# Attention beside a feed-forward block on one core: a list planner's prices for GpSimd, its rule for row slices and its rule string are changed

## The chip, the cores and the metric

The kernel runs on one core of one Trainium2 chip. The metric is the device time of one execution, in microseconds; the time of before is the median of three runs. The engines are called as the profile calls them: PE (TensorE) with its weight loads PEld, ACT (ScalarE), DVE (VectorE), POOL (GpSimd) and SP (SyncE, which here issues nearly all transfers).

## What is computed

`x` is 2048 tokens of 640 values. The output is the sum of `x`, a multi-query attention over the normalised `x` (32 heads of 20 values that share one key and one value projection) and a feed-forward block of width 1728 over the same normalised `x`.

```python
def _A_ref(x, wq, wk, wv, wo):
    q = (lambda x, *d: x.transpose(*d))((x @ wq).reshape(B, S, H, Dh), 0, 2, 1, 3)
    k = x @ wk
    v = x @ wv
    scores = jnp.einsum("bhqd,bkd->bhqk", q, k) * (Dh ** -0.5)
    p = _softmax(scores, axis=-1)
    o = jnp.einsum("bhqk,bkd->bhqd", p, v)
    return (lambda x, *d: x.transpose(*d))(o, 0, 2, 1, 3).reshape(B, S, H * Dh) @ wo
def _B_ref(x, w1, w2):
    h = jnp.einsum("bsd,df->bsf", x, w1)
    h = _silu(h)
    out = jnp.einsum("bsf,fd->bsd", h, w2)
    return out
...
xn = _layernorm(x, axis=-1)
return x + _A_ref(xn, A_wq, A_wk, A_wv, A_wo) + _B_ref(xn, B_w1, B_w2)
```

## The kernel before

**Tiles.** The queries are cut into 4 chunks of 512 tokens and the 32 heads into 8 groups of 4, which gives 32 groups of work; in each, 16 tiles of 128 keys meet 4 heads of 512 queries. A score tile (`s_mm`, L1045) is one matmul of 32 rows by 128 columns into one PSUM bank; four of them, one for each head, can run side by side in the four row slots of the array. The weighted sum over the keys (PV, `pv_mms`, L1165) is four matmuls of 128 rows by 32 columns side by side, into bank 7. Weights times activations (queries, hidden layer, output) are column cuts in the same manner (`col_mm`, L427): four matmuls for one set. A **row slice** (`row_mm`, L434) is another way to do a quarter of such a set: one matmul of 32 rows by 128 columns that goes into a row slot which a score set leaves empty; four slices replace one column set.

**Two ways to the exponential.** ACT takes two or three banks of scores at a time with its exponential (L1130). For some key tiles of a group, a "batch" (`claim`, L1255), DVE and POOL do it instead: DVE adds a bias and rounds the scores into the bits of a bf16 number (p1, L1326, once for each head), and two copies shifted by constants are made of the four heads' result at once, a first shift s1 and a second s2. The second is always POOL's (L1365), the first is POOL's if its backlog is under `pj`, and else DVE's (L1370). Three PV sets with three versions of the values sum the three copies. So a batch takes 4 heads' tiles from ACT and adds two PV sets.

**The rest.** After the last key tile of a group the sums in bank 7 are copied out (L1213), their last row is turned round by transfers and a reciprocal (L820), POOL multiplies (the normalise, L829), and transfers pack the result. The query projections, the hidden layer (a tanh on ACT, L749, and a product on DVE, L752) and the output blocks (L871, and y at L886 for the last chunk) are fitted in between. At the end stand the sum (L966), its reciprocal (L969), the spread (L984), the product (L993), the last part of the output projection (`fin_job`, `fin_b`) and its eviction (L934).

**What sets the order.** Nothing is ordered by hand. `build` runs a list planner on the host with a clock for each engine: `Sched.est` gives the earliest start of an operation from what it depends on, `Sched.way` the time from the end of one operation to the start of another on a second engine, `Sched.commit` advances the clocks and the transfers' queue. An operation has a price `occ` on its engine and a latency `lat`. `port` marks the POOL operations and DVE shifts that share a memory port: `est` lets neither start before the other's `port_free`. The order that comes out is written to the engines with semaphores; on the chip each engine then runs its own list strictly in order. `step_pe` ranks PE's candidates; `row_slice` offers a slice only where the rule `ru.rows` allows a cut to be opened. Every 10 us of planned time (`PIECE`) one letter of the string `PLAN` chooses a deviation from the settings in `BASE` (`RULES`). The planner runs before the launch; none of its time is in the metric.

The prices that matter here, in ns: `POOL_SHIFT` 1900 for a shift and the default latency 60; 1350 + 200 for the normalise; 240 from POOL to PE; 600 or so for a p1.

Of the kernel before, what the change touches and what calls it, by code (L numbers as in the profile page):

```python
# [12 lines left out]
ALU = mybir.AluOpType  # L13

P = 128
D = 640
# [5 lines left out]
NG = H // HG  # L22
# [24 lines left out]
HALF = 320  # L47

LAT = 70.0
WAY = {("act", "dve"): 145.0, ("dve", "pool"): 10.0, ("pool", "pe"): 240.0}  # L50
WAY_E = 130.0
WAY_U = -50.0
WAY_DMA = -130.0
WAITS = 0.0
BUSY = 0.5
STRETCH = 2400.0
# [12 lines left out]
NG1 = 3  # L69
PA = 0.3  # L70
LOOKP = 1.0
POOL_SHIFT = 1900.0
POOL_J = (2,)
SWITCH = 85.0
SPRIO = 0.5
# [5 lines left out]
MARGIN = 200.0  # L81
# [9 lines left out]
ACT_LN = (5, 7)  # L91
TRACT = (0, 1)

BASE = dict(hold2=0, bnd=4, pj=4000.0, rows=1, rowmin=3, lagmax=6, lagp=0, lagj=6, openlag=5, late=-0.02, lead=0.01, leadmax=0.02, need=460.0, hold=300.0, dwant=600.0, slack=550.0, dnow=400.0, hungry=0.0, patience=0.0, keep=460.0, open=2, zcap=9, stay=0.0, homes=1, want=1, claim=6)
RULES = dict(a={}, b=dict(keep=0.0), c=dict(lagp=3), d=dict(lagp=5), e=dict(lagp=0), f=dict(patience=200.0), g=dict(dwant=0.0),
             h=dict(zcap=4), i=dict(zcap=3), j=dict(homes=0), k=dict(leadmax=-1.0, lead=-1.0), l=dict(lead=0.08, leadmax=0.1),
             m=dict(need=560.0), n=dict(hold=0.0), o=dict(stay=460.0), p=dict(open=1), q=dict(slack=400.0), r=dict(hungry=1000.0), s=dict(claim=9), t=dict(open=3), u=dict(claim=4), v=dict(want=2), w=dict(slack=700.0), x=dict(hold2=4), y=dict(bnd=0), z=dict(pj=-1e9), A=dict(rows=0), B=dict(rows=2, rowmin=2), C=dict(pj=2000.0), D=dict(openlag=3), E=dict(pj=8000.0), F=dict(hold2=3))
PLAN = "aaatadFcxxttxFzxBrtrAzgngmztnFaqEAEDaAqzirfDaaytFxFxrapAtznvqvndtnao"


def rule(n):
# [98 lines left out]
class Sched:  # L200
# [30 lines left out]
    def way(self, h, op):  # L231
        if h.eng == op.eng:
            return 0.0
        if h.dma_sem is not None:
            return WAY_DMA
        if op.eng == "pe" and op.mode == "p":
            if h.eng == "act":
                return WAY_E
            if h.eng == "dve" and h.name.startswith("Ucopy"):
                return WAY_U  # L240
        return WAY.get((h.eng, op.eng), LAT)

# [27 lines left out]
    def commit(self, op, start):  # L270
        e = op.eng
        op.deps = self.hazards(op)
        if op.sync is not None:
            op.deps.add(op.sync)
        op.start = start
        if e == "pe":
            if op.mode != self.pe_mode:
                start += SWITCH + (30.0 if op.mode == "p" else 20.0 if op.mode == "f" else 0.0)
                self.pe_mode = op.mode
            s0 = self.joined(op)  # L280
            if s0 is not None:
                end = max(start + op.occ, self.pe_set[2])
                self.pe_set = (s0, self.pe_set[1] | op.slots, end)
                op.fin = start + op.occ + 170.0
                op.occ = end - self.t[e]
                self.t[e] = end
            else:
                op.fin = start + op.occ + 170.0
                self.t[e] = start + op.occ
                self.pe_set = (start, op.slots, start + op.occ) if op.slots else None  # L290
        elif e == "sp":
            self.t[e] = start + op.occ
            own = 3300.0 if op.name == "dma wv" else 800.0 if op.name.startswith("dma pk") else 2000.0 if op.name.startswith("dma la") else 0.0
            self.dma_free = max(self.dma_free, start + 1300.0) + (op.lat - 800.0 if op.name.startswith("dma pk") else op.lat)
            op.fin = self.dma_free + 700.0 + own
        else:
            op.fin = start + op.occ + op.lat
            self.t[e] = start + op.occ
            if op.port:
                self.port_free[e] = start + op.occ  # L300
        op.done = True
        for r in op.reads:
            r.r.append(op)
        for r in op.writes:
            r.w = op
            r.r = []
        self.order[e].append(op)
        if op.on_commit is not None:
            op.on_commit(op)


def build(nc, A_x, A_wq, A_wk, A_wv, A_wo, B_x, B_w1, B_w2, out, stack):
    S = A_x.shape[1]
    F = B_w1.shape[1]
# [41 lines left out]
    U_sb = sb([P, 2, QW], F32)  # L356
# [7 lines left out]
    Rrep = nblk[:, 0:QW]  # L364
# [55 lines left out]
    def pool(fn, occ, lat=60.0, **kw):  # L420
        return sc.add(Op("pool", fn, occ, lat, **kw))
# [40 lines left out]
    def load_x(n):  # L462
# [12 lines left out]
               prio=0.04)  # L475
# [322 lines left out]
    pack_op = {}  # L798
# [12 lines left out]
    def norm_job(g, uc):  # L811

        qc, gi = divmod(g, NG)
        us, par = g % 2, qc % 2
        u0 = U_sb[DH:DH + 1, us, :]
        pu = u0.ap[0][0]
        la = dma(f"la{us}", lambda e: e.dma_start(
            Lg[:, us, :], bass.AP(U_sb, u0.offset, [[pu * SLOT, HG], [HG * QW // P, SLOT], [1, HG * QW // P]])), 8192,
            pre=[uc], reads=[res("U", us)], writes=[res("Lg", us)], prio=0.5)
        rc = dve(lambda v: v.reciprocal(rLg[:, us, :], Lg[:, us, :]), 160, pre=[la], reads=[res("Lg", us)],  # L820
                 writes=[res("rLg", us)], prio=0.1, name="recip")
        lb = dma(f"lb{us}", lambda e: e.dma_start(
            bass.AP(nblk, Rrow.offset, [[4 * Rrow.ap[0][0], HG], [HG * QW // P, SLOT], [1, HG * QW // P]]), rLg[:, us, :]),
                 8192, pre=[rc] + spread_op.get(g - 1, []), reads=[res("rLg", us)], writes=[res("Rrow")], prio=0.5)
        lc = [dma(f"lc{us}", lambda e, h=h: e.dma_start(Rrep[h * SLOT:(h + 1) * SLOT, :],
                                                        bass.AP(nblk, Rrow[4 * h:4 * h + 1, :].offset, [[Rrow.ap[0][0], 1], [0, SLOT], [1, QW]])),
                  5 * SLOT * QW * 4, pre=[lb] + [un_op[k] for k in [g - 1] if k in un_op], reads=[res("Rrow")], writes=[res("Rrep", h)], prio=0.5) for h in range(HG)]
        spread_op[g] = lc
        nm = pool(lambda e: e.tensor_tensor(oU[:, us, :], U_sb[:, us, :], Rrep, ALU.mult), 1350.0 + MARGIN, pre=[uc] + lc + pack_op.get(divmod(g - 2, NG), []),  # L829
                  reads=[res("U", us)] + [res("Rrep", h) for h in range(HG)], writes=[res("oU", us)], prio=0.1)  # L830
        un_op[g] = nm
        nm.port = True
        nm.gate = calm(nm)
        packs = []
        for i in range(HG):
            row = (gi * HG + i) * DH
            lo = i * SLOT
            left = DH
            while left:
                c, r = divmod(row, P)  # L840
                n = min(left, P - r)
                o = dma(f"pk{us}", lambda e, c=c, r=r, n=n, lo=lo: e.dma_start(oT[r:r + n, par, c, :], oU[lo:lo + n, us, :]),
                        n * QW * 2 + 200000, pre=[nm] + ([kT_op[k] for k in range(KT)] + q_op[0] if qc == 1 else []), reads=[res("oU", us)], writes=[res("oT", par, gi, i, c)], prio=0.6)
                o.gate = lambda: oT_free(qc)
                packs.append(o)
                row, lo, left = row + n, lo + n, left - n
        pack_op[(qc, gi)] = packs
# [203 lines left out]
    def plan(n):  # L1051
# [17 lines left out]
        if w[2] is None or w[2][0] < need - ru.hold:  # L1069
# [3 lines left out]
    RUNLIST = {k: [tuple(range(a, a + (k - 1) * d + 1, d)) for d in range(1, STEPS + 1) for a in range(UB - (k - 1) * d)]  # L1073
               for k in (2, 3)}

    def left_over(banks, gone):

        return sum(all(b in banks and b not in gone for b in r) for r in RUNLIST[3])

    e_owner = [None] * NSLOT  # L1080
    e_next = [0]
# [255 lines left out]
    def dve_advance(job):  # L1337
# [14 lines left out]
        for j in range(1, NJ):  # L1352
# [10 lines left out]
            args = dict(pre=st["p1"] + ([idb] + [norm_op[n] for n in range(NT)] if old is None else [old] if isinstance(old, Op) else [old["pv"][j]]), reads=zr, writes=[r], name=f"s{j}")  # L1363
            if j in POOL_J or pool_load() < ru.pj:
                op = pool(lambda v, t=t, j=j, zin=zin: v.tensor_scalar(t.bitcast(I16), zin, float(SHIFT[j]), 1.0, ALU.add, ALU.mult),  # L1365
                          POOL_SHIFT, prio=0.3, **args)
                op.port = True
                op.gate = calm(op)
            else:
                op = dve(lambda v, t=t, j=j, zin=zin: v.tensor_scalar_add(t.bitcast(I16), zin, float(SHIFT[j])), t_dve(N, 4),  # L1370
                         prio=SPRIO - 0.01 * j, **args)
                op.port = True
                op.on_commit = shifts.append
# [354 lines left out]
    def dve_idle(t):  # L1728
# [3 lines left out]
                return False  # L1732
        return True

    def lag_now():
        pend = [n for n in e_users if exp_ops[n].done and any(o is None or not o.done for o in e_users[n])]
        return att["n"] - min(pend) if pend else 0

    def step_pe():
        t = sc.t["pe"]  # L1740
# [40 lines left out]
        if ru.stay and mode != "s" and not pro and t + 230.0 < act_until(att["n"]) - ru.stay:  # L1781
            order.remove("s")
            order.insert(len(order) - 1, "s")
        if not make_s_act() and all(not u for u in unclaimed):
            order = ["p", "pd", "d", "r", "m0", "m", "l", "s"]
        order += ["z", "x"]
        if ru.bnd and att["pgroup"] < NGR and pv_left[att["pgroup"]] <= ru.bnd and not pro:
# [268 lines left out]
```

## Time and profile before

| | before |
|---|---|
| median of 3 runs, us | 700.38 (699.88 to 700.77) |
| the profiled execution, us | 700.23 |
| its span, first to last instruction, us | 698.3 |
| granted TensorE clock | 1.00 throughout |
| read from HBM, written to HBM | 11.09 MB, 2.62 MB |

In the profile's groups a row holds the line, the engine, the operation, output and input with their shapes and the count; then the busy time in us and the mean ns of one; then the idle time just before the group's instructions, with what ended it. A stretch's row holds the busy us of PE, PEld, DVE, ACT and POOL, each with its count of instructions, then the clock, the transfers' share and GB/s. A row of the waits is "who waited <- for whom: us in total, times, longest". A timeline row is the start, the length from the first start to the last end, and what ran how often. An instruction's duration runs to the end of its last write, so on ACT, DVE and PE the next one may start before it ends.

### The profile page before, as it was taken

What the parts mean: (1) busy time and instruction counts of PE and PEld (TensorE: products, weight loads), DVE (VectorE), ACT (ScalarE), POOL (GpSimd) and SP (SyncE); (2) the same over time, 40 slices, a digit from 0 to 9 for tenths busy, and PEclk for the clock granted to TensorE, in tenths of its full rate; (3) what the DMA queues carried; (4) which work ended last, traced back from release to release, by engine and by line L of the source; (5) the groups of instructions that cost most, each with busy time, mean ns of one, the idle gap of its engine ahead of it and who ended that gap; (6) DMA issues with size and microseconds to landing.
All of it is one profiled execution on the core that took longest, in us unless ns stands there. A gap on an engine that the chain in (4) does not pass through costs nothing.

```text
span 698.3 us, 22678 instructions
## 1 busy us (share of the span) xinstructions
PE 683.0 (98%) x9927; PEld 228.4 (33%) x9927; DVE 572.4 (82%) x969; ACT 679.4 (97%) x735; POOL 584.4 (84%) x351
## 2 busy tenths in 40 slices
PE   8999999999999999999999999999999999999997
PEld 5422222222232433322223333322223233333344
DVE  7788788899898668988898888788899798778763
ACT  6899999999999999999999999999999999999994
POOL 6658999989985976989988679999888997999991
PEclk9999999999999999999999999999999999999999
DMA  7643220222211222231122221232222022232201
GB/s 219 186 163 41 19 21 22 31 28 28 22 14 18 38 39 33 35 65 18 23 22 29 29 29 24 30 74 30 28 19 22 9 31 32 32 67 22 23 7 40
DMA packets 34242, 28.99 MB, mean 42 GB/s; under 512 B 15486, under 2 KB 29662, under 8 KB 34142
## 3 DMA queue, kind: packets, MB, share of 16 engines
q1 hardware_dynamic: 33854, 27.20, 25.3%
q8 instruction: 78, 1.28, 0.8%
q10 hardware_dynamic: 288, 0.33, 0.1%
q14 instruction: 22, 0.18, 0.1%
HBM read 11.09 MB, written 2.62 MB: 20 GB/s over the span
## 4 chain that ended last, share of the span: by engine, by line
PE 43%; ACT 42%; POOL 7%; DVE 5%; DMA 2%; issue 1%; SPq 0%; DVEq 0%; POOLq 0%; ACTq 0%
ACT sbt L1130 40%; PE psall L1165 15%; PE psall L1045 14%; PE psall L427 12%; POOL sbt L1365 7%; DVE sbt L1326 2%; ACT sbt L749 2%; DVE sbt L1370 1%; DMA sbt<-in_A_x_dram 1%; DMA sbt<-sbt 1%; PE psall L601 1%; DVE sbt L934 0%; PE psall L966 0%; DVE sbt L1213 0%; PE psall L984 0%
## 5 line engine op out<-in xcount | busy, mean ns | idle before, releaser
L1130 ACT ACTIVATE sbt<-psall 128x1024 bf16<-128x1024 f32 (+1 forms) x663 | 657.6, 1215 | 3.0 <-PE psall L1045 2.3
L1365 POOL TENSOR_SCALAR sbt<-sbt 128x2048 int16<-128x2048 int16 x275 | 521.7, 1897 | 76.1 <-DVE sbt L1326 25.3
L1326 DVE TENSOR_SCALAR sbt<-psall 128x512 int16<-128x512 f32 x648 | 427.1, 684 | 90.5 <-PE psall L1045 74.5
L1045 PE MATMUL psall<-sbt 32*128 32x512 bf16 x2048 | 271.6, 385 | 4.5 <-ACT sbt L1130 1.3
L1165 PE MATMUL psall<-sbt 128*32 128x512 bf16 x3344 | 270.7, 385 | 4.0 <-POOL sbt L1365 1.5
L427 PE MATMUL psall<-sbt 128*32 128x320 bf16 (+3 forms) x3664 | 221.4, 331 | 0.3 <-DVE sbt L1326 0.2
L1045 PEld LDWEIGHTS psall<-sbt 32*128 32x128 bf16 x2048 | 72.0, 91 | 248.0 <-ACT sbt L1130 190.7
L1165 PEld LDWEIGHTS psall<-sbt 128*32 128x32 bf16 x3344 | 66.4, 94 | 120.7 <-issue 82.1
L427 PEld LDWEIGHTS psall<-sbt 128*32 128x32 bf16 (+1 forms) x3664 | 79.9, 95 | 76.3 <-issue 45.7
L434 PE MATMUL psall<-sbt 32*128 32x320 bf16 (+1 forms) x240 | 81.4, 339 | 0.4
L829 POOL TENSOR_TENSOR sbt<-sbt 128x512 bf16<-128x512 f32 x30 | 38.2, 1274 | 11.6 <-DVE sbt L1370 6.6
L1370 DVE TENSOR_SCALAR sbt<-sbt 128x2048 int16<-128x2048 int16 x49 | 43.1, 894 | 0.6 <-PE psall L1165 0.5
L752 DVE SCALAR_TENSOR_TENSOR sbt<-sbt,psall 128x512 bf16<-128x512 bf16 x52 | 35.5, 683 | 6.8 <-ACT sbt L749 5.7
L749 ACT ACTIVATE sbt<-psall 128x512 bf16<-128x512 f32 x52 | 39.4, 757 | 0.1
L434 PEld LDWEIGHTS psall<-sbt 32*128 32x128 bf16 x240 | 21.8, 91 | 2.9 <-PE psall L434 2.1
L1213 DVE COPY sbt<-psall 128x512 f32<-128x512 f32 x31 | 21.2, 682 | 0.5 <-PE psall L1165 0.3
L1638 PE MATMUL psall<-sbt 128*32 128x256 bf16 (+1 forms) x296 | 19.8, 365 | 1.2 <-DVE sbt L467 1.2
L672 DVE TENSOR_SCALAR sbt<-psall 128x512 bf16<-128x512 f32 x20 | 13.7, 683 | 1.1 <-PE psall L434 0.5
L871 DVE SCALAR_TENSOR_TENSOR sbt<-psall,sbt 128x320 bf16<-128x320 f32 x24 | 11.6, 481 | 0.6 <-PE psall L1045 0.6
L565 POOL TENSOR_SCALAR sbt<-sbt 128x640 bf16<-128x640 bf16 x12 | 10.4, 874 | 1.7 <-DVE sbt L557 1.4
L552 POOL TENSOR_TENSOR sbt<-sbt 128x2 f32<-128x2 f32 x8 | 5.5, 693 | 6.7 <-DVE sbt L550 6.7
L1638 PEld LDWEIGHTS psall<-sbt 128*32 128x32 bf16 x296 | 8.1, 110 | 6.8 <-issue 3.2
(63 smaller groups left out, 110.6 us busy)
## 6 DMA issues: line engine op xcount, KB each, us to landing
sbt<-sbt SPq DMA_DIRECT2D x120, 64.0 KB, 3.9
sbt<-in_A_x_dram SPq DMA_DIRECT2D x28, 160.0 KB, 3.9
sbt<-sbt SPq DMA_DIRECT2D x213, 20.0 KB
out_dram<-sbt SPq DMA_DIRECT2D x14, 160.0 KB, 3.0
sbt<-in_B_w_dram SPq DMA_DIRECT2D x1, 2160.0 KB, 11.7
sbt<-in_B_w_dram SPq DMA_DIRECT2D x1, 2080.0 KB, 8.3
sbt<-sbt SPq DMA_DIRECT2D x75, 8.0 KB
sbt<-in_A_wq_dram SPq DMA_DIRECT2D x1, 800.0 KB, 7.5
```

The costliest lines, as they stand in the source:

```text
L427: ins = pe.matmul(ps[j * SLOT:(j + 1) * SLOT, b * BANK + off:b * BANK + off + n], w[:, j * SLOT:(j + 1) * SLOT], x, start=start, stop=stop ...
L434: return pe.matmul(ps[0:w.shape[-1], b * BANK:b * BANK + n], w[k], x[k], start=start, stop=stop, tile_position=(r * SLOT, 0))
L749: t = Op("act", lambda a: a.activation(t_buf[0:rows, ts, :], bk(job.bank, 0, QW, rows=rows), AF.Tanh, scale=0.5), t_act(512), 215, pre=[jo ...
L752: u = Op("dve", lambda v: v.scalar_tensor_tensor(out=hT[par][0:rows, fk, :], in0=t_buf[0:rows, ts, :], scalar=1.0, in1=bk(job.bank, 0, QW, ...
L829: nm = pool(lambda e: e.tensor_tensor(oU[:, us, :], U_sb[:, us, :], Rrep, ALU.mult), 1350.0 + MARGIN, pre=[uc] + lc + pack_op.get(divmod(g ...
L1045: return pe.matmul(bk(b), kT_rep[i * SLOT:(i + 1) * SLOT, kt * P:(kt + 1) * P], qT[i * SLOT:(i + 1) * SLOT, g % NQ, :], start=True, stop=T ...
L1130: return a.activation(Ebuf[:, es * QW:es * QW + w], ps[:, buf[0] * BANK:buf[0] * BANK + w], AF.Exp, scale=ESCALE)
L1165: ins = pe.matmul(ps[i * SLOT:(i + 1) * SLOT, UB * BANK:UB * BANK + QW], lhsT, rhs, start=(first and k < HG), stop=(last and k >= len(lst) ...
L1326: p1 = Op("dve", lambda v: v.tensor_scalar(z16[:, i * QW:(i + 1) * QW], bk(job.bank), ZBIAS, 0.0, ALU.add, ALU.max), t_dve(QW) + 2.0, 140, ...
L1365: op = pool(lambda v, t=t, j=j, zin=zin: v.tensor_scalar(t.bitcast(I16), zin, float(SHIFT[j]), 1.0, ALU.add, ALU.mult), POOL_SHIFT, prio=0 ...
L1370: op = dve(lambda v, t=t, j=j, zin=zin: v.tensor_scalar_add(t.bitcast(I16), zin, float(SHIFT[j])), t_dve(N, 4), prio=SPRIO - 0.01 * j, **args)
L1638: ins = pe.matmul(ps[i * SLOT:(i + 1) * SLOT, UB * BANK:UB * BANK + n], zero_t[:, 0:SLOT], zero_t[:, 0:n], start=fresh, stop=fresh, tile_p ...
```

## The change

The planner's prices for POOL are replaced: a shift 1976 without latency in place of 1900 with 60, the normalise 1356 in place of 1550, 160 from POOL to a PV or column set (`WAY_S`) in place of 240 to any PE operation. The shared port counts as free 79 ns (`PORT_GAP`) before a POOL operation's slot ends, and a DVE operation that waited for the port is 53 ns (`PORT_HID`) cheaper. In `BASE`, `rows` goes from 1 to 0, so that slices are offered only in stretches whose letter is `B` (as before, two open cuts) or the new `G` (one), and `pj` goes from 4000 to 6000. `PLAN` is another string of 68 letters, with 8 `B` and 3 `G`. `left_over`, `lag_now` and one test in `step_pe` are written to run faster on the host.

```diff
-WAY = {("act", "dve"): 145.0, ("dve", "pool"): 10.0, ("pool", "pe"): 240.0}
+WAY = {("act", "dve"): 145.0, ("dve", "pool"): 10.0}
...
+WAY_S = 160.0
+PORT_GAP = 79.0
+PORT_HID = 53.0
...
-POOL_SHIFT = 1900.0
+POOL_SHIFT = 1976.0
...
-BASE = dict(hold2=0, bnd=4, pj=4000.0, rows=1, ...
+BASE = dict(hold2=0, bnd=4, pj=6000.0, rows=0, ...
...
-...  F=dict(hold2=3))
-PLAN = "aaatadFcxxttxFzxBrtrAzgngmztnFaqEAEDaAqzirfDaaytFxFxrapAtznvqvndtnao"
+...  F=dict(hold2=3), G=dict(rows=1))
+PLAN = "aaanGtxBBExhEhmxadrBBzraCBBEGqtrztfFzrqhwnpofocotyxddmGjvmpBaBitntqo"
...
         if op.eng == "pe" and op.mode == "p":
             if h.eng == "act":
                 return WAY_E
+            if h.eng == "pool":
+                return WAY_S
...
+            if op.port and e == "dve" and start > self.t[e] and start <= self.port_free["pool"] + 1.0:
+                op.occ -= PORT_HID
             op.fin = start + op.occ + op.lat
             self.t[e] = start + op.occ
             if op.port:
-                self.port_free[e] = start + op.occ
+                self.port_free[e] = start + op.occ - (PORT_GAP if e == "pool" else 0.0)
...
-        nm = pool(lambda e: e.tensor_tensor(oU[:, us, :], U_sb[:, us, :], Rrep, ALU.mult), 1350.0 + MARGIN, ...
+        nm = pool(lambda e: e.tensor_tensor(oU[:, us, :], U_sb[:, us, :], Rrep, ALU.mult), 1356.0, ...
...
-                          POOL_SHIFT, prio=0.3, **args)
+                          POOL_SHIFT, 0.0, prio=0.3, **args)
...
-        pend = [n for n in e_users if exp_ops[n].done and any(o is None or not o.done for o in e_users[n])]
-        return att["n"] - min(pend) if pend else 0
+        n, base = att["n"], lag_base[0]
+        while base < n and exp_ops[base].done and all(o is not None and o.done for o in e_users[base]):
+            base += 1
+        lag_base[0] = base
+        for k in range(base, n):
+            if exp_ops[k].done and any(o is None or not o.done for o in e_users[k]):
+                return n - k
+        return 0
```

What the two built programs hold, counted by instruction; every other instruction, each transfer among them, is there as often in both, and nearly all stand in another order from about the 40th microsecond on:

| instruction (line before) | before | after |
|---|---|---|
| ACT exponential of 2 banks, of 3 banks (L1130) | 589, 74 | 573, 82 |
| DVE p1 (L1326) | 648 | 656 |
| DVE first shifts (L1370) | 49 | 49 |
| POOL first shifts, second shifts (L1365) | 113, 162 | 115, 164 |
| PE row slices of 320 columns, of 512 (L434) | 136, 104 | 32, 28 |
| PE column matmuls of 320 columns, of 512 (L427) | 2184, 1372 | 2288, 1448 |
| PE matmuls of PV (L1165) | 3344 | 3360 |
| PE fillers of 256 columns, of 512 (L1638) | 156, 140 | 148, 116 |

More of the change, by code (lines that the diff above doesn't have):

```diff
@@ L92 @@
 TRACT = (0, 1)
-BASE = dict(hold2=0, bnd=4, pj=4000.0, rows=1, rowmin=3, lagmax=6, lagp=0, lagj=6, openlag=5, late=-0.02, lead=0.01, leadmax=0.02, need=460.0, hold=300.0, dwant=600.0, slack=550.0, dnow=400.0, hungry=0.0, patience=0.0, keep=460.0, open=2, zcap=9, stay=0.0, homes=1, want=1, claim=6)
+BASE = dict(hold2=0, bnd=4, pj=6000.0, rows=0, rowmin=3, lagmax=6, lagp=0, lagj=6, openlag=5, late=-0.02, lead=0.01, leadmax=0.02, need=460.0, hold=300.0, dwant=600.0, slack=550.0, dnow=400.0, hungry=0.0, patience=0.0, keep=460.0, open=2, zcap=9, stay=0.0, homes=1, want=1, claim=6)
 RULES = dict(a={}, b=dict(keep=0.0), c=dict(lagp=3), d=dict(lagp=5), e=dict(lagp=0), f=dict(patience=200.0), g=dict(dwant=0.0),
              h=dict(zcap=4), i=dict(zcap=3), j=dict(homes=0), k=dict(leadmax=-1.0, lead=-1.0), l=dict(lead=0.08, leadmax=0.1),
-             m=dict(need=560.0), n=dict(hold=0.0), o=dict(stay=460.0), p=dict(open=1), q=dict(slack=400.0), r=dict(hungry=1000.0), s=dict(claim=9), t=dict(open=3), u=dict(claim=4), v=dict(want=2), w=dict(slack=700.0), x=dict(hold2=4), y=dict(bnd=0), z=dict(pj=-1e9), A=dict(rows=0), B=dict(rows=2, rowmin=2), C=dict(pj=2000.0), D=dict(openlag=3), E=dict(pj=8000.0), F=dict(hold2=3))
-PLAN = "aaatadFcxxttxFzxBrtrAzgngmztnFaqEAEDaAqzirfDaaytFxFxrapAtznvqvndtnao"
+             m=dict(need=560.0), n=dict(hold=0.0), o=dict(stay=460.0), p=dict(open=1), q=dict(slack=400.0), r=dict(hungry=1000.0), s=dict(claim=9), t=dict(open=3), u=dict(claim=4), v=dict(want=2), w=dict(slack=700.0), x=dict(hold2=4), y=dict(bnd=0), z=dict(pj=-1e9), A=dict(rows=0), B=dict(rows=2, rowmin=2), C=dict(pj=2000.0), D=dict(openlag=3), E=dict(pj=8000.0), F=dict(hold2=3), G=dict(rows=1))
+PLAN = "aaanGtxBBExhEhmxadrBBzraCBBEGqtrztfFzrqhwnpofocotyxddmGjvmpBaBitntqo"
 def rule(n):
@@ L828, in norm_job @@
         spread_op[g] = lc
-        nm = pool(lambda e: e.tensor_tensor(oU[:, us, :], U_sb[:, us, :], Rrep, ALU.mult), 1350.0 + MARGIN, pre=[uc] + lc + pack_op.get(divmod(g - 2, NG), []),
+        nm = pool(lambda e: e.tensor_tensor(oU[:, us, :], U_sb[:, us, :], Rrep, ALU.mult), 1356.0, pre=[uc] + lc + pack_op.get(divmod(g - 2, NG), []),
                   reads=[res("U", us)] + [res("Rrep", h) for h in range(HG)], writes=[res("oU", us)], prio=0.1)
@@ L1074, in build @@
                for k in (2, 3)}
+    RUN3 = [frozenset(r) for r in RUNLIST[3]]
     def left_over(banks, gone):
-        return sum(all(b in banks and b not in gone for b in r) for r in RUNLIST[3])
+        left = set(banks).difference(gone)
+        return sum(r <= left for r in RUN3)
     e_owner = [None] * NSLOT
@@ L1733, in dve_idle @@
         return True
+    lag_base = [0]
     def lag_now():
-        pend = [n for n in e_users if exp_ops[n].done and any(o is None or not o.done for o in e_users[n])]
-        return att["n"] - min(pend) if pend else 0
+        n, base = att["n"], lag_base[0]
[6 more added lines that the diff above has]
+        return 0
     def step_pe():
@@ L1783, in step_pe @@
             order.insert(len(order) - 1, "s")
-        if not make_s_act() and all(not u for u in unclaimed):
+        if all(not u for u in unclaimed) and not make_s_act():
             order = ["p", "pd", "d", "r", "m0", "m", "l", "s"]
```

## Prediction

> **What bounds the kernel now.** I read the page's head first, then the groups of instructions by line with shapes apart, the busy time by stretches, the table of waits, and the timeline where a price was wanted.
>
> ```profile
> span 698.3 us, 22678 instructions
> PE 683.0 (98%) x9927; PEld 228.4 (33%) x9927; DVE 572.4 (82%) x969; ACT 679.4 (97%) x735; POOL 584.4 (84%) x351
> ...
> 400.00:500.00 100.00, 99.31 (x1478) 32.41 (x1478) 81.95 (x133) 100.00 (x108) 89.69 (x50) 1.00 0.27 37
> ...
> L1130 ACT ACTIVATE sbt<-psall 128x1024 bf16<-128x1024 f32 x589 | 571.8, 1170 | 1.9 <-PE psall L1045 1.2
> L1130 ACT ACTIVATE sbt<-psall 128x1536 bf16<-128x1536 f32 x74 | 113.8, 1578 | 1.2 <-PE psall L1045 1.1
> ...
> PEld psall L1045 <- ACT sbt L1130: 190.7, 501, 0.8
> PEld psall L1165 <- issue: 82.1, 364, 0.2
> ```
>
> Two engines look full. PE's 98% is spread over pipelined matmuls, so it doesn't say that PE is the limit. The waits decide: 501 times the weight load of a score set (L1045) stood until ACT's exponential (L1130) gave up PSUM banks, 190.7 us in all. Even a wait that nothing causes ("issue") lasts 82.1/364 = 0.226 us, the change of tile shape; without it about 190.7 - 501 x 0.226 = 77 us are left in which PE had nothing to do but wait for ACT. ACT, on the other hand, is busy in every us of the stretch from 400 to 500. ACT sets the pace from the first exponential to the last.
>
> But "busy" on ACT counts an instruction's latency too; the mean of 1170 ns is not the step from one to the next. That step comes from the timeline of ACT:
>
> ```profile
> 13.93 5.98 ACT sbt L1130 x5
> ...
> 86.86 3.07 ACT L1130 ACTIVATE sbt<-psall 128x1024 bf16<-128x1024 f32 x3
> 89.58 0.85 ACT L749 ACTIVATE sbt<-psall 128x512 bf16<-128x512 f32 x1
> 90.05 2.21 ACT L1130 ACTIVATE sbt<-psall 128x1024 bf16<-128x1024 f32 x2
> 91.86 0.89 ACT L749 ACTIVATE sbt<-psall 128x512 bf16<-128x512 f32 x1
> ...
> 680.26 8.35 ACT L1130 ACTIVATE sbt<-psall 128x1536 bf16<-128x1536 f32 x6
> ```
>
> A pair of banks takes (91.86 - 90.05)/2 = 0.905 us, a tanh (L749) 0.47. Three banks: (8.35 - 1.58)/5 = 1.354 from this row, 0.905 + (1.578 - 1.170) = 1.313 from the two means; I take 1.33. From the first exponential (13.93) to the end of the last (680.26 + 8.35 = 688.61) are 674.7 us. The steps add to 589 x 0.905 + 74 x 1.33 + 54 x 0.47 + about 2 for the three projections = 658.9. So ACT loses about 15.8 us to late score sets, a loss that the idle column (1.9 + 1.2) hardly shows. The span is: 13.9 before, 658.9 of steps, 15.8 of loss, 9.7 behind.
>
> **ACT's work (the two more batches).** By the built order ACT issues 573 pairs and 82 triples: -16 x 0.905 + 8 x 1.33 = **-3.8 us**, on the path. This is the surest term. Eight heads' tiles move to DVE and GpSimd (on GpSimd 162 to 164 second shifts and 113 to 115 first ones; DVE keeps 49 shifts), whose prices are:
>
> ```profile
> 133.00 15.73 POOL L1365 TENSOR_SCALAR sbt<-sbt 128x2048 int16<-128x2048 int16 x8
> 656.05 2.47 DVE L1326 TENSOR_SCALAR sbt<-psall 128x512 int16<-128x512 f32 x4
> L1365 POOL TENSOR_SCALAR sbt<-sbt 128x2048 int16<-128x2048 int16 x275 | 521.7, 1897 | 76.1 <-DVE sbt L1326 25.3 <-DVE sbt L1370 16.9 <-PE psall L1165 8.1
> L1370 DVE TENSOR_SCALAR sbt<-sbt x49: 673/820/2328, 54.9 to 661.4; 128x2048 int16<-128x2048 int16 x49
> ```
>
> GpSimd's step is (15.73 - 1.90)/7 = 1.976 us, so four more shifts are +7.9; DVE's is (2.47 - 0.68)/3 = 0.60, so eight more first passes are +4.8. Both lie beside ACT: GpSimd has 698 - 584 = 114 us idle, DVE 126. Were that cover gone, as in the stretch at 133 where GpSimd runs eight shifts without a gap, a late shift holds the PV matmul that wants it and with it all that is queued on PE.
>
> **PE (slices only by rule).** 180 row slices of 1 matmul go, 26 + 19 column cuts of 4 matmuls come.
>
> ```profile
> 661.21 0.39 PE L1045 MATMUL psall<-sbt 32*128 32x512 bf16 x3
> 661.22 0.30 PE L434 MATMUL psall<-sbt 32*128 32x320 bf16 x1
> 661.53 0.40 PE L1165 MATMUL psall<-sbt 128*32 128x512 bf16 x4
> ...
> 666.19 1.05 PE L1165 MATMUL psall<-sbt 128*32 128x512 bf16 x16
> 680.02 1.13 PE L427 MATMUL psall<-sbt 128*32 128x320 bf16 x28
> ```
>
> The slice starts 10 ns after the score set and is over before it: it costs PE nothing, and taking it away frees nothing. The cuts cost stream time: (1.05 - 0.40)/3 = 0.217 us for 4 matmuls of 512 columns, hence 0.137 for 320. So 26 x 0.137 + 19 x 0.217 = +7.7; 16 more PV matmuls +0.9; 8 fewer fillers of 256 and 24 of 512 columns -1.5; 654 contiguous stretches of score work become 649, each some 0.44 (0.32 to the next kind, as 661.21 to 661.53, and 0.12 back), -2.2. Net +4.9 us for PE, which lies under the 77 us of waiting for ACT on the average; without that cover it would be all on the path.
>
> **The tail.** The built order puts the last y blocks behind the last exponentials, so more of the final projection (L427) is left behind the last spread (L984): 124 matmuls for 72.
>
> ```profile
> 690.97 1.05 PE L984 MATMUL psall<-sbt 128*32 128x128 f32 x32
> 691.84 2.77 PE L427 MATMUL psall<-sbt 128*32 128x512 bf16 x72
> 692.59 3.08 DVE L934 SCALAR_TENSOR_TENSOR sbt<-psall,sbt 128x512 bf16<-128x512 f32 x5
> ```
>
> At 0.217 us for 4 x 512 columns the 124 stream 4.6 us (9 sets each of 512, 384 and 256, 4 of 128), the 72 stream 2.5. PE ends at 691.84 + 2.77 = 694.6 and the last eviction starts at 692.59 + 4 x 0.6 = 695.0; 2.1 later on PE makes that 696.7: **+1.7**. Bounds 0 (if those matmuls fill waits for L969 and L993) and +2.1.
>
> **The loss of 15.8 us.** The new numbers (1.976 for the shift, the port free 79 ns before its slot ends, 1.356 for the normalise, 160 ns to PE) stand close to the rows: 1.976, 1.976 - 1.897 = 0.079. The old 1.900 was short by 76 ns a shift, and the trace has what follows:
>
> ```profile
> PEld psall L1165 <- POOL sbt L1365: 12.5, 37, 0.8
> PE psall L1165 <- POOL sbt L1365: 1.5, 5, 0.4
> 658.12 0.10 PEld L1165 LDWEIGHTS psall<-sbt 128*32 128x32 bf16 x4 [0.62 <-POOL sbt L1365]
> ```
>
> Of 14.0 us in 42 waits, 42 x 0.226 are the change of shape; 4.5 us are GpSimd being late, the most that better numbers can give back there. The other bound is +7.7: every new column cut in a place where PE has no lead. Counted in the two built orders with the prices above, score sets whose stretch of PE work outlasts the exponential it lies under are 199 before and 184 after, so I stay near the first bound: **-2**. The planner's quicker counting of lag and runs changes nothing that runs; transfers are as many as before. The first 40 us are ordered as before but for a few PE rows.
>
> Sum: -3.8 + 1.7 - 2 = -4.1 us on 700.23 us of the profiled execution (span 698.3 and 1.9 around it), 0.15 under the median of the runs shown, 700.38. Forecast **696.3 us**, -0.6%.
>
> **Rules of the Trainium skill.** The L1370 row has shifts on DVE from 673 to 2328 ns for one shape, and a run that began beside a GpSimd shift shows why: DVE stands until it ends. The Trainium skill (SBUF — State Buffer, Who interferes with whom) says that whichever of the two issues first holds the shared ports for its whole instruction and the other fully blocks, so issue order decides, not a constant in the planner. The trace agrees in the 2328 ns. By that rule alone the 53 ns that the new planner takes off such a wait would be worth nothing, and the collision rival below takes the place of my -2.
>
> PE's row of 98% would, taken at its word, put the +4.9 us on the path. The Trainium skill (Perfetto Trace Analysis, Identifying the Most-Contended Engine) says that matmul busy time is no good measure for TensorE, and to use the load of weights' share; that is 33% here. By the row (PE the limit, ACT's saving worth nothing) the sum would be 4.9 + 1.7 = +6.6, by the rule -4.1.
>
> **Rivals.**
> - *The stalls go.* All 4.5 us of GpSimd's lateness vanish from ACT's loss: -3.8 + 1.7 - 4.5 = -6.6, 693.8 us. For it: the 76 ns. Against: PE waits for ACT at 501 of some 650 sets, so most lateness on PE is taken up there.
> - *No gain left.* The plan is new in nearly all of its 68 stretches, and the loss grows by about 2 elsewhere: -3.8 + 1.7 + 2 = -0.1, 700.3 us. The change then doesn't do what it says.
> - *Column cuts on the path (slower).* A slice went under a score set for nothing; as a column cut it stands between two score sets. If two thirds of 7.7 fall where PE has no lead, -3.8 + 1.7 + 5.1 = +3.0, 703.4 us. It decides from 2.1/7.7 = 27% on. For it: 0.905 us for a pair leaves only 0.905 - 0.44 = 0.46 for two PV sets or three cuts. Against: the 77 us.
> - *Collisions (slower).* A DVE shift that meets a GpSimd shift head-on costs 2.33 - 0.67 = 1.66 us, less one exponential of lead (0.9) is 0.75 on ACT. Ten more of these in the new order: -3.8 + 1.7 + 7.5 = +5.4, 705.8. DVE issues 49 shifts as before, which speaks against it.
>
> **Chances.** Forecast 0.48, the stalls go 0.12, no gain left 0.15, column cuts 0.18, collisions 0.07. Less than 0.2% (1.4 us) can't be told from no change by these measurements. So faster 0.60, same 0.15, slower 0.25. The forecast's own range is 693.5 (loss -4.5, tail +1.6) to 699 (loss +0.5, tail +2.1). The whole range goes from 691, where some lateness of DVE goes too, to 703.5, which takes in the column cuts and leaves out the collisions.
>
> **What would show it.** ACT with 573 + 82 exponentials and steps of 0.905 and 1.33 between them; about 669 us from the first exponential to the end of the last where it had 674.7; the last exponential's end to the end of the span 11.4 where it had 9.7; fewer than 42 waits of L1165's counterpart for GpSimd. I am wrong if the sum of ACT's steps falls by 3.8 and the stretch doesn't: then the loss has grown, and the waits in front of the score sets name the engine; or if the tail grows by more than 2.1.

## The result and the profile after

The changed kernel takes 693.92 us in the median (four runs, 693.9 to 694.29) where the kernel before took 700.18 beside it: ratio 0.9911, 95% interval 0.9894 to 0.9928, or 6.3 us less. 696.3 was forecast, within a range of 691.0 to 703.5; the time lies closest to the rival in which GpSimd's lateness goes (693.8).

The page of the changed kernel, its head and the groups that answer to those of before (L1140 is L1130 of before, L1375 is L1365):

```profile
span 692.1 us, 22655 instructions
...
PE 680.5 (98%) x9908; PEld 229.7 (33%) x9911; DVE 572.0 (83%) x977; ACT 673.5 (97%) x727; POOL 593.0 (86%) x355
...
L1375 POOL TENSOR_SCALAR sbt<-sbt 128x2048 int16<-128x2048 int16 x279 | 530.5, 1901 | 62.7 <-DVE sbt L1380 12.7
```

The row of DVE's own shifts alone (count, then the least, median and longest duration in ns; L1370 of before had 673/820/2328):

```profile
L1380 DVE TENSOR_SCALAR sbt<-sbt x49: 630/697/2065, 64.3 to 654.1; 128x2048 int16<-128x2048 int16 x49
```

The groups by line with shapes apart, then the table of waits:

```profile
L1140 ACT ACTIVATE sbt<-psall 128x1024 bf16<-128x1024 f32 x573 | 555.0, 1172 | 0.3
...
L1140 ACT ACTIVATE sbt<-psall 128x1536 bf16<-128x1536 f32 x82 | 124.6, 1555 | 1.9 <-PE psall L1052 1.7
```

```profile
PEld psall L1052 <- ACT sbt L1140: 194.9, 503, 0.8
...
PEld psall L1175 <- POOL sbt L1375: 9.5, 35, 0.6
```

ACT still sets the pace: 503 score sets waited for it, as before 501. PV waits for GpSimd 35 times and 9.5 us where it was 42 times and 14.0; beyond 0.226 us for each change of shape that is 1.6 us, down from 4.5. GpSimd does four more shifts and idles 62.7 us before them where it idled 76.1. The median of DVE's own shifts fell from 820 to 697 ns: 17 of the 49 took over 0.8 us where 26 did, so fewer of them stood long behind a GpSimd shift.

Next come rows from ACT's timeline at both ends of the exponentials, then the chip's end from the timeline of all engines:

```profile
12.84 2.37 ACT L1140 ACTIVATE sbt<-psall 128x1536 bf16<-128x1536 f32 x2
...
676.59 4.31 ACT L1140 ACTIVATE sbt<-psall 128x1536 bf16<-128x1536 f32 x3
```

```profile
683.97 4.82 PE L434 MATMUL psall<-sbt 128*32 128x384 bf16 x124
685.23 1.36 DVE L941 SCALAR_TENSOR_TENSOR sbt<-psall,sbt 128x512 bf16<-128x512 f32 x2 [0.59 <-PE psall L434]
687.20 0.69 DVE L941 SCALAR_TENSOR_TENSOR sbt<-psall,sbt 128x512 bf16<-128x512 f32 x1 [0.60 <-PE psall L434]
688.19 1.34 DVE L941 SCALAR_TENSOR_TENSOR sbt<-psall,sbt 128x512 bf16<-128x512 f32 x2 [0.30 <-PE psall L434]
```

The exponentials end at 676.59 + 4.31 = 680.90, which leaves 11.2 us of tail where 9.7 were. The 124 matmuls take 4.82 us behind the spread (2.77 for 72 before), and DVE now waits for PE three times among the five evictions (0.59, 0.60 and 0.30 us), where it ran five without a gap.

The span can be cut as the prediction cut it: the start of the first exponential; ACT's steps (0.905 for a pair, 1.33 for a triple, 0.47 for a tanh, 2 for the projections); what the stretch from the first to the end of the last exponential holds beyond them, the loss; the tail, from there to the end of the span. All kernels of this study side by side, in us (the steps of the two kernels with act16 are those of before less 3.8; each ratio is to runs of before made beside that kernel). The intervals reach 0.0009 to 0.0017 to either side, 0.6 to 1.2 us, so a smaller difference between two rows is not shown by the times alone.

| kernel | median, or ratio to before [95%] | span | first | steps | loss | tail | PV's waits for GpSimd's shifts (PEld) |
|---|---|---|---|---|---|---|---|
| before | 700.18 | 698.3 | 13.9 | 658.9 | 15.8 | 9.7 | 12.5 in 37 |
| after | 0.9911 [0.9894, 0.9928] | 692.1 | 12.8 | 655.0 | 13.1 | 11.2 | 9.5 in 35 |
| b_shift490 | 0.9968 [0.9956, 0.9979] | 695.7 | 13.0 | 658.9 | 14.0 | 9.7 | 3.9 in 17 |
| a_shift490 | 0.9911 [0.9896, 0.9926] | 691.8 | 13.0 | 655.0 | 12.6 | 11.2 | 3.6 in 16 |
| b_shift256 | 0.9970 [0.9958, 0.9982] | 695.6 | 12.9 | 658.9 | 14.1 | 9.7 | 2.5 in 11 |
| a_shift256 | 0.9906 [0.9892, 0.9921] | 691.8 | 13.3 | 655.0 | 12.3 | 11.2 | 5.0 in 22 |
| b_slice64 | 0.9999 [0.9990, 1.0009] | 698.1 | 13.1 | 658.9 | 16.3 | 9.8 | |
| a_tail | 0.9903 [0.9888, 0.9918] | 691.4 | 13.1 | 655.0 | 12.9 | 10.4 | |
| a_cols | 0.9892 [0.9877, 0.9907] | 690.4 | 12.9 | 655.0 | 11.5 | 11.1 | |
| b_cols | 0.9981 [0.9972, 0.9991] | 696.5 | 12.8 | 658.9 | 15.1 | 9.7 | |
| b_act16 | 0.9989 [0.9980, 0.9999] | 697.3 | 13.1 | 655.1 | 19.3 | 9.7 | 15.5 in 41 |
| b_act16_shift490 | 0.9924 [0.9907, 0.9941] | 693.7 | 13.1 | 655.1 | 15.8 | 9.7 | 4.3 in 18 |
| p_newprices | 1.0058 [1.0042, 1.0074] | 702.2 | 13.0 | 662.3 | 15.7 | 11.2 | 7.5 in 29 |
| p_oldprices | 1.0203 [1.0186, 1.0220] | 712.6 | 12.8 | 664.0 | 26.2 | 9.6 | 22.0 in 59 |

From before to after the span falls by 6.2: first -1.1, steps -3.9, loss -2.7, tail +1.5. The first term isn't the plan's: in the profile of before ACT stood 1.00 us for a transfer of x ahead of its first statistics, in no other. The run b_slice64, as long as before, began at 13.1 and lost 16.3, so about half of that 1.1 only moves into the loss.

### The profile page after: what moved, and what is told of

Read it like the earlier page. It is cut to its first block, busy times and chain, and to the rows that moved or that the text cites. A ratio compares the mean times of both kernels' runs of the same rounds, so it can differ in the third digit from the quotient of the medians.

```text
span 692.1 us, 22655 instructions
## 1 busy us (share of the span) xinstructions
PE 680.5 (98%) x9908; PEld 229.7 (33%) x9911; DVE 572.0 (83%) x977; ACT 673.5 (97%) x727; POOL 593.0 (86%) x355
## 4 chain that ended last, share of the span: by engine, by line
ACT 57%; PE 35%; DVE 5%; POOL 3%; issue 1%; DMA 0%
ACT sbt L1140 53%; PE psall L434 11%; PE psall L1175 11%; PE psall L1052 11%; ACT sbt L756 3%; POOL sbt L1375 2%; DVE sbt L1336 1%; DVE sbt L552 1%; DVE sbt L550 1%; DVE sbt L594 1%; POOL sbt L836 0%; DMA sbt<-in_A_x_dram 0%; PE psall L608 0%; PE psall L973 0%; DVE sbt L679 0%
## 5 line engine op out<-in xcount | busy, mean ns | idle before, releaser
L1140 ACT ACTIVATE sbt<-psall 128x1024 bf16<-128x1024 f32 (+1 forms) x655 | 652.5, 1220 | 2.2 <-PE psall L1052 1.7
L1375 POOL TENSOR_SCALAR sbt<-sbt 128x2048 int16<-128x2048 int16 x279 | 530.5, 1901 | 62.7 <-DVE sbt L1380 12.7
L1052 PE MATMUL psall<-sbt 32*128 32x512 bf16 x2048 | 265.9, 384 | 3.7 <-ACT sbt L1140 1.8
L1175 PE MATMUL psall<-sbt 128*32 128x512 bf16 x3360 | 267.7, 384 | 1.2 <-DVE sbt L1223 0.4
L434 PE MATMUL psall<-sbt 128*32 128x320 bf16 (+2 forms) x3844 | 226.6, 331 | 0.7 <-ACT sbt L1140 0.5
L1052 PEld LDWEIGHTS psall<-sbt 32*128 32x128 bf16 x2048 | 70.0, 91 | 248.8 <-ACT sbt L1140 194.9
L434 PEld LDWEIGHTS psall<-sbt 128*32 128x32 bf16 x3844 | 83.9, 95 | 77.7 <-issue 46.9
L1175 PEld LDWEIGHTS psall<-sbt 128*32 128x32 bf16 x3360 | 66.0, 94 | 115.1 <-issue 82.4
L1380 DVE TENSOR_SCALAR sbt<-sbt 128x2048 int16<-128x2048 int16 x49 | 39.8, 827 | 0.2
L441 PE MATMUL psall<-sbt 32*128 32x320 bf16 (+1 forms) x60 | 20.5, 342 | 0.1
L893 DVE SCALAR_TENSOR_TENSOR sbt<-psall,sbt 128x320 f32<-128x320 f32 x8 | 3.9, 485 | 9.8 <-PE psall L434 9.7
L572 POOL TENSOR_SCALAR sbt<-sbt 128x640 bf16<-128x640 bf16 x12 | 10.4, 878 | 1.5 <-DVE sbt L564 1.2
L1648 PEld LDWEIGHTS psall<-sbt 128*32 128x32 bf16 x264 | 7.3, 113 | 6.2 <-issue 3.4
```

The source lines that it names most:

```text
L434: ins = pe.matmul(ps[j * SLOT:(j + 1) * SLOT, b * BANK + off:b * BANK + off + n], w[:, j * SLOT:(j + 1) * SLOT], x, start=start, stop=stop ...
L1052: return pe.matmul(bk(b), kT_rep[i * SLOT:(i + 1) * SLOT, kt * P:(kt + 1) * P], qT[i * SLOT:(i + 1) * SLOT, g % NQ, :], start=True, stop=T ...
L1140: return a.activation(Ebuf[:, es * QW:es * QW + w], ps[:, buf[0] * BANK:buf[0] * BANK + w], AF.Exp, scale=ESCALE)
L1175: ins = pe.matmul(ps[i * SLOT:(i + 1) * SLOT, UB * BANK:UB * BANK + QW], lhsT, rhs, start=(first and k < HG), stop=(last and k >= len(lst) ...
L1648: ins = pe.matmul(ps[i * SLOT:(i + 1) * SLOT, UB * BANK:UB * BANK + n], zero_t[:, 0:SLOT], zero_t[:, 0:n], start=fresh, stop=fresh, tile_p ...
```

## Experiments

Kernels beginning with b_ or a_ keep the order of before or of after, instruction by instruction, and change what one kind of instruction does; they leave a part of the arithmetic out. Those beginning with p_ let the planner make another order.

**Is GpSimd's lateness in the loss, and is it less in the new order?** Every shift on GpSimd covers fewer columns of each head:

```diff
-op = pool(lambda v, t=t, j=j, zin=zin: v.tensor_scalar(t.bitcast(I16), zin, ...
+w = 490 if (j, wi) in used else QW
+used.add((j, wi))
+tv = t if lent else t.rearrange("p (h q) -> p h q", h=HG)
+zv = z16.rearrange("p (h q) -> p h q", h=HG)
+op = pool(lambda v, tv=tv[:, :, 0:w], j=j, zv=zv[:, :, 0:w]: v.tensor_scalar(tv.bitcast(I16), zv, ...
```

> The order of before, each GpSimd shift (after the first on a tile) over 4 x 490 of its 4 x 512 columns, the last 22 of each head keep what stood there: 88 x 0.926 = 81 ns less, so the chip's step of 1.976 us becomes 1.895, what the old planner had assumed. Theory A (the old price was short, and that is why the loss of 15.8 us was larger than now): 696.5 to 698 us, and the waits of PV for GpSimd fall from 14.0 us in 42 to under 10 us in 35. Rival B (lateness of GpSimd is taken up by PE's waiting for ACT, the new order is only a better string): 699.5 to 700.2.

> The order of after with the same cut of every GpSimd shift. Theory A: this order was laid out for 1.976 us, so 81 ns less free little: 693.2 to 693.9 us. Rival B: what holds for the order of before holds here, both fall by the same amount.

> The order of before, each GpSimd shift (after the first on a tile) over 4 x 256 columns, the rest keeps what stood there: some 1.03 us a step, GpSimd is never late. Theory A: all of its part of the loss goes, 695 to 697 us, and waits of PV for GpSimd under 2 us beyond the 0.226 us of each change of shape. Rival B: 698.5 to 700.

> The order of after with the same halving. Theory A: the 1.6 us that waits for GpSimd last beyond the change of shape (9.5 us in 35) bound it, 692.3 to 693.5 us, so the two orders come to lie 3 to 4 us apart instead of 6.3 (ACT's steps -3.8, tail +1.5, the rest of the loss). Rival B: the distance of 6.3 us stays.

The group of shifts in the first of these kernels (by line, shapes apart):

```profile
L1371 POOL TENSOR_SCALAR sbt<-sbt 128x1960 int16<-128x1960 int16 x269 | 490.8, 1824 | 80.8 <-DVE sbt L1326 21.3 <-DVE sbt L1376 21.1 <-PE psall L1165 10.6
```

A shift took 1824 ns for 1897: 73 less, so its step is 1.90 us, what the old planner reckoned with. That alone gives the order of before 0.32%, 2.3 us (697.38 beside 699.66); the order of after gains nothing clear of the noise (693.48 against 693.92, and a ratio of 0.9911 for both). Halving the shift, to 1043 ns, gives no more (697.75 and 693.27; at most 697 was expected of the first). So the theory holds for the price: GpSimd's 76 ns cost the old order 2.3 us, and the new order, laid out for 1.976, at most 0.7. But it explains only a part: the two orders, 6.3 us apart, still stand 3.9 to 4.5 us apart, so 1.8 to 2.4 us of the gain come in this way.

The shorter shift frees DVE too. The row of DVE's shifts in the same kernel:

```profile
L1376 DVE TENSOR_SCALAR sbt<-sbt x49: 652/683/1404, 54.5 to 658.8; 128x2048 int16<-128x2048 int16 x49
```

Their median is 683 ns where it was 820, and PV waits for them 1.2 us in 4 times where it waited 4.0 in 12 (table of waits). How much of the 2.3 us came by this way, and how much by GpSimd's own shifts being ready sooner, was not separated.

**Do row slices or column cuts cost PE anything that counts?**

```diff
 # b_slice64
-op.fn = lambda pe: row_mm(pe, job.bank, n, w, v, r, *op.ends)
+op.fn = lambda pe: row_mm(pe, job.bank, 64, w, v[:, 0:64], r, *op.ends)
 # a_cols, b_cols
-... col_mm(pe, b, n, w, x, *op.ends)
+... col_mm(pe, b, n, w, x, *op.ends) if op.ends[0] else col_mm(pe, b, n * 3 // 4, w, x[:, 0:n * 3 // 4], *op.ends)
```

> The order of before, each of its 240 row slices over 64 columns instead of 320 or 512 (the rest of that quarter of the sum is left out). Theory A (a slice lies under the score set beside it and costs nothing): within 0.7 us of before, 699 to 700.4. Rival (slices hold up the score set or the change of shape, and their removal is a part of the gain): 696.5 to 698.5.

> The order of after; every column set of a query, hidden or output job but the first of each job runs over 3/4 of its columns (the rest of those sums is left out): some 30 us less for PE. Theory A (ACT sets the pace, PE's work counts only where it outlasts the exponential it lies under): 689 to 692 us, at most 5 us less. Rival (PE is the bound, as its 98% says): 675 us or less.

> The same for the order of before. Theory A: 2 to 5 us less than before, 695 to 698, and no further from before than a_cols is from after by more than 1.5 us. Rival (the 45 new column cuts cost the order of after several us that it wins elsewhere): a_cols gains 3 us or more beyond what this one gains.

Slices of 64 columns instead of 320 or 512 change nothing (0.9999); to leave them out altogether was not tried. A quarter off nearly all column sets, an estimated 32 to 34 us of PE's stream by the prediction's 0.137 and 0.217 us a set, gives 1.6 us in the new order (692.31 against 693.92) and 1.2 in the old one (698.53 against 699.71); both lie just outside the range expected, and as ratios both gain 0.0019. PE's bound of 98% is refuted. The rival of the column cuts did not come, and the two orders gain alike, so the new one does not suffer more from its cuts; at 1.6 us for 34 the 7.7 us that it adds would cost 0.4 us, an estimate, for the 45 cuts were not taken out by themselves.

```profile
PE 665.6 (96%) x9911; PEld 230.4 (33%) x9911; DVE 573.0 (83%) x977; ACT 672.7 (97%) x727; POOL 592.2 (86%) x355
```

In a_cols (head of the page) PE's busy time falls only by 15 us, and by the table of waits the score sets' waits for ACT grow from 194.9 us in 503 to 203.3 in 523.

**Is the longer tail the matmuls behind the last spread?** In `o_mms` and `fa` of banks 0, 1 and 3:

```diff
+if cut and c != chunks[0]:  # in o_mms; fa in the same manner
+    return pe.matmul(ps[0:SLOT, b * BANK + off:b * BANK + off + 64], oT[0:n, qc % 2, c, i * P:i * P + SLOT],
+                     wo_sb[0:n, c, e0:e0 + 64], start=False, stop=False, tile_position=(0, 0))
```

> The order of after; in the final projection of banks 0, 1 and 3 each set after the first of its piece is one matmul of 64 columns instead of four of up to 512 (that part of the sum is left out), which takes about 1.6 us of PE from behind the last spread. Theory A (the tail's 11.2 us from the end of the last exponential are longer than the 9.7 of before by these matmuls): 692.2 to 692.8 us, tail 9.6 to 10.2. Rival (the tail is the chain of sum, reciprocal, spread and eviction): no change, 693.5 to 694.

About half: the tail falls from 11.2 to 10.4, the time by 0.8 to 693.16, which is less than was expected and within the noise of the ratios (0.9903 for 0.9911), so it rests on the tail of the trace. The rest stands behind what DVE still waits for, as the timeline of this kernel shows:

```profile
684.74 2.01 DVE L948 SCALAR_TENSOR_TENSOR sbt<-psall,sbt 128x512 bf16<-128x512 f32 x3
...
687.44 1.34 DVE L948 SCALAR_TENSOR_TENSOR sbt<-psall,sbt 128x512 bf16<-128x512 f32 x2 [0.69 <-PE psall L434]
```

The first three evictions now follow without a gap; the last two wait 0.69 us for PE, on the sets of banks 2 and 4, which were not cut. The weight loads of PE's last 48 matmuls there had themselves waited 0.57 us for an eviction, so with the cut DVE holds up PE too, and the 0.8 us need not be all that the matmuls cost.

**Do ACT's steps count one to one, as the prediction's surest term had it?**

```diff
+if len(buf) == 2 and todo and n >= todo[0]:
+    wc = 740
+    todo.pop(0)
...
+todo = [40 * k for k in range(1, 17)]
...
-return a.activation(Ebuf[:, es * QW:es * QW + w], ps[:, buf[0] * BANK:buf[0] * BANK + w], AF.Exp, scale=ESCALE)
+return a.activation(Ebuf[:, es * QW:es * QW + wc], ps[:, buf[0] * BANK:buf[0] * BANK + wc], AF.Exp, scale=ESCALE)
```

> The order of before; 16 of its 589 exponentials of two banks, spread over the run, take 740 of their 1024 columns (the rest keeps what stood there): 16 x 284 columns are 3.8 us of ACT's steps, as much as the new order saves. Theory A (ACT's steps stand on the path one to one): 3 to 3.8 us less than before, 696 to 697. Rival (PE, DVE or GpSimd takes over what ACT gives): less than 1.5 us less, 698.4 to 699.7.

> The order of before with both: the 16 shorter exponentials and the GpSimd shifts of 4 x 490 columns. Theory A (the two terms add): 5 to 6 us less than before, 694 to 695 us, which is the order of after but for its longer tail (+1.5) and the rest of its smaller loss. Rival (with ACT's steps shorter, GpSimd's lateness counts for more or for less): under 694 or over 695.5.

Not in the old order. 3.8 us off ACT's steps give the order of before 0.6 us (0.9989), and the loss grows from 16 to 19.3. Two things eat it. First, the score set behind a shortened exponential is not there yet, since PE's list is unchanged: of the steps after the 16 short ones only three were the least possible 666 to 667 ns, the mean was 820, which returns 16 x 0.153 = 2.4 us on the spot; four of the 16 were late in before already (926 to 1061 ns) and gained next to nothing. Second, as it seems, GpSimd (the last column of the table).

With ACT quicker PV waits more for GpSimd, 15.5 us for 12.5. With GpSimd's shift at 1.90 us as well, the same edit on ACT brings another 2.6 us (697.38 to 694.83; the two were timed beside runs of before of 699.66 and 699.88). Alone the two edits are worth 2.3 and 0.6, together 5.1; if they added, the ratio would be 0.9957, which lies outside the interval of 0.9907 to 0.9941. So the theory's number for both (694 to 695) held, its reason, that the terms add, didn't. The edit is not the change, though: it shortens single exponentials and leaves the order around them, while the change takes whole tiles from ACT and orders anew. It was not tried on the order of after.

**Which half of the change brings the gain?** Both kernels start from after: p_newprices puts the string, `rows` and `pj` of before back, p_oldprices the prices (the normalise's 1350 + 200 and the 240 to every PE operation too).

```diff
 # p_newprices
-BASE = dict(hold2=0, bnd=4, pj=6000.0, rows=0, ...
+BASE = dict(hold2=0, bnd=4, pj=4000.0, rows=1, ...
-PLAN = "aaanGtxBBExhEh...
+PLAN = "aaatadFcxxttxF...
 # p_oldprices
-WAY_S = 160.0
-PORT_GAP = 79.0
-PORT_HID = 53.0
-POOL_SHIFT = 1976.0
+WAY_S = 240.0
+PORT_GAP = 0.0
+PORT_HID = 0.0
+POOL_SHIFT = 1900.0
...
-POOL_SHIFT, 0.0, prio=0.3, **args)
+POOL_SHIFT, prio=0.3, **args)
```

> The new prices alone: GpSimd's durations, port and ways of after, with the rule string, rows = 1 and pj = 4000 of before. The planner then makes another order: 584 pairs and 80 triples, so 3.5 us more of ACT's steps than before, and 116 matmuls behind the last spread, some 1.3 us more tail. Theory A (the prices cut GpSimd's lateness, but ACT's steps come from the string that was fitted to them): 701.5 to 704 us, with under 40 waits of PV for GpSimd. Rival (the prices alone bring the gain): 698 us or less.

> The new rules and the new string with the old prices for GpSimd (1900 + 60 for a shift, 1550 for the normalise, 240 to PE, nothing for the port). Another order comes out: 577 pairs and 86 triples, 5 fewer batches than in after, so 5.1 us more of ACT's steps than before; the tail has a little less left behind the last spread than before. Theory A (string and prices are fitted to each other, and neither half of the change gains by itself): 703 to 711 us, and again over 40 waits of PV for GpSimd. Rival (the string and the rules carry the gain, the prices are a detail): 698 us or less.

Neither: 704.25 us (1.0058) and 714.42 (1.0203), 0.25 and 3.4 us over the expected ranges. Under the new prices and the old string PV waits for GpSimd only 29 times and 7.5 us, yet the loss is 15.7 as in before: fewer such waits are not by themselves a smaller loss. That order also has 3.4 us more of ACT's steps and a longer tail. The new string under the old prices is the worst of all, with 59 waits for GpSimd (22.0 us) and a loss of 26.2. From its table of waits:

```profile
ACT sbt L1140 <- PE psall L1052: 11.0, 15, 2.8
```

Here ACT itself stands 11.0 us for score sets (1.7 in after). Each of the two is one order, with counts of its own, so they show that neither half alone brings the gain, and not what each half is worth.

## Why the prediction was right, and where not

What the prediction said would show it came about: the stretch from the first exponential to the end of the last is 680.90 - 12.84 = 668.1 us where about 669 was said, the tail 11.2 for 11.4, and PV's waits for GpSimd are fewer than 42.

- *What bounds the kernel.* Right that PE's stream doesn't: a_cols and b_cols take over 30 us from it and give 1.6 and 1.2 us. That ACT does is read from its waits and rows; b_act16 shows that ACT's steps alone don't set the time either.
- *ACT's steps, -3.8.* The size stands in the trace: 573 and 82 exponentials, -3.9 by the same prices. "On the path" and "the surest term" were too sure as a reason: on the old order 3.8 us of steps gave 0.6, and 2.6 with GpSimd's shift at its price. So the steps count as far as score sets and shifts come earlier too. That they do in the new order is read from the cut span, where the loss did not grow; no run takes this term alone.
- *GpSimd's and DVE's extra work at nothing.* Right for the amounts (GpSimd's idle time fell from 76.1 to 62.7 and PV's waits for it fell all the same). That this hangs on the prices is not shown: p_oldprices has 22.0 us of such waits, but in another order.
- *PE's +4.9 under its waits.* Right as far as tried: shorter slices free nothing (0.9999), and a quarter off the columns gives both orders the same 0.0019.
- *The tail, +1.7.* +1.5 measured. a_tail gives 0.8 of it back; that the rest lies in the sets of banks 2 and 4 is read from DVE's waits and wasn't tried.
- *The loss, -2.* Mis-sized: -2.7, or -3.2 from b_slice64, which starts nearly when after does. The shortened shifts put 1.8 to 2.4 us of the gain down to GpSimd's price. The rest was not separated. A rough reading of the traces follows each late exponential back through PE's work to the last wait for another engine. It ends at a GpSimd shift for some 2 us of the loss in before and under 1 in after (next to nothing in p_newprices, some 9 in p_oldprices). The largest part, some 9 us in before and 7 in after, ends at ACT itself: PE's work since ACT gave up the banks outlasted the exponential. As far as this reading goes the new order also places PE's work better, as the prediction's 199 and 184 sets had it; what in the string does this stays open.
- *The rule on the shared ports.* DVE's shifts still range from 630 to 2065 ns (673 to 2328 before), so single head-on collisions go on, as the Trainium skill (SBUF — State Buffer, Who interferes with whom) says; but their median fell by 123 ns, and the rival in which they grow didn't come. The 53 ns, which the prediction held to be worth nothing by that rule alone, are in the trace. In before 18 of DVE's shifts met no GpSimd instruction and took 673 to 695 ns. Of the 31 that began during one, 29 ended 545 to 549 ns after it, however long they had stood. The planner's price for such a shift is 598 ns (`t_dve`), and 598 less 53 is 545. What the 53 ns alone do for the time was not tried.

The forecast of -4.1 thus had the direction and the terms, and was 2.2 us short of 6.3: about 1 in the loss, and the rest in the start of the one profile of before, from which the sum was made, and in the scatter of the runs. That the sum came out so near is in part luck, since its surest term did not stand by itself.

## What to carry to other kernels

A price that is 76 ns short on an engine that is busy for 84% of the span costs little by itself (2.3 us of 700 here), but in this order it also took most of what was saved on the engine that sets the pace (of 3.8 us 0.6 came through, and 2.6 with the price met): the two should be costed together. A string of rules and the prices under which a planner reads it can't be judged apart: here either half alone was slower, by 0.6 and 2.0%. And the loss of a bound engine should be measured by its steps from start to start, since idle time behind overlapping latencies showed 3 us where 16 were lost.

## What the runs showed of the hardware

A GpSimd shift of 1024 columns took 1043 ns, one of 1960 took 1824 and one of 2048 took 1897, so a column costs 0.83 ns; where a shift follows without waiting it starts 79 ns after the end of the last. In before a DVE shift that had to stand for GpSimd ended 545 to 549 ns after it (29 of 31), where one that met nothing took 673 to 695 ns: some 130 ns of it lie in the wait. The kernel's 240 row slices beside score sets cost the same at 64 columns as at 320 and 512 (0.9999). A quarter off nearly all column sets shortened PE's busy time by 15 us only, half of the estimated stream that it took away; why was not tried.
